# A gMLP and linear-attention block on one NeuronCore: the spatial matmul u = w_sp z2 by Strassen's seven products over half of the source tiles

## The chip, the cores and the metric

The kernel runs on one core of a Trainium2 chip. The metric is the device time in microseconds (us), here that of the one core, as the median of several runs. The core has five engines that matter here, each with its own queue of instructions worked off in order: PE (TensorE, matmuls; its weight loads are shown apart as PEld), DVE (VectorE), ACT (ScalarE), POOL (GpSimd) and SP (SyncE), which in this kernel issues the DMA transfers. An instruction starts when those ahead of it on its engine are through and the semaphores it waits for have arrived.

## The reference

The block has two halves: linear attention over 2048 tokens with 512 features, then a gated MLP that mixes tokens. Both add to the token stream x, with shifts, scales and gates from a condition. The change lies in the second half:

```python
S, D, F = 2048, 512, 1376; Fh = F // 2          # 688
z  = gelu(einsum("bsd,df->bsf", x, w_in))
z1 = z[..., :Fh]
z2 = layernorm(z[..., Fh:], axis=-1)
g  = einsum("ts,bsf->btf", w_sp, z2) + b_sp[None, :, None]
y  = einsum("bsf,fd->bsd", z1 * g, w_out)
...
x = x + gb * y
```

`w_sp` is 2048 x 2048 in tokens, so g is a 2048 x 2048 by 2048 x 688 product, the largest of the block.

## The kernel before

Tokens are cut into 16 tiles of 128 (NT), the 688 features of z2 into two halves of 344 (HB). The kernel computes in fp32 by splitting each operand into a high part of the type fp32r and a low part, the remainder, and by adding three matmuls: high x high, high x low, low x high. The helper `hi_lo` makes them: ACT copies into the high part (L83), and DVE or POOL subtracts it from the source for the low part (L84). `mm3` issues the three output matmuls (L66 to L68).

The first 349 us compute the attention half and z. Their instructions stand in an order of some hundreds of named steps (the string ORDER) that `run_all` works off; it ends with the z2 tiles and the first splits of w_sp. z1 goes to a DRAM buffer (z1d) and the token stream to another (x1d); z2 stays in SBUF, one tile of [128, 2, 688] (high, low) for each token tile (`Z2`).

Then comes the w_sp stage, a loop over the 16 target tiles. For target tile i, `sp_mm` (L769) multiplies, for all 16 source tiles s, the 128 x 128 block w_sp[i, s] (transposed in the input, split in groups of four blocks by `split_wsp`) with z2 of tile s: three matmuls for each half of the features, 96 of 344 columns in all, into one PSUM tile of two banks that stays open for the whole sum. `u_out` (L780) adds the bias and multiplies with z1 on DVE. `u_x` (L809) cuts the result into two uint16 planes on ACT (L194) and sends them through a transposing DMA; `u_e` (L814) puts the planes together on DVE (L204) and splits high (ACT, L818) and low parts (DVE, L819, L820). `wout_mm` (L842) multiplies with w_out in 17 matmuls of 512 columns, and `out_store` (L837) adds the token stream on DVE and stores. In the loop the output product of tile i-1 stands behind the w_sp matmuls of tile i, and `load3(i + 1)`, `u_e(i - 1)` and the splits of w_sp's tile i+1 in the middle of them (L847 to L888). The last tile is transposed on PE (`u_t`, L789) in place of the DMA, between two pieces of the output product of tile 14.

w_out itself is prepared in iteration 0: `load_wout` fetches six pieces, `split_wout` (L755) multiplies each with the gate on DVE (L757) and splits it on ACT and POOL.

SBUF comes from fixed pools, each a ring of equal buffers: `ws` 2 of 5504 fp32, `zs` 16 of 1376 (the z2 tiles), `s4` 8 of 1024 (split w_sp), `md` 4, `ta` 6, `tb` 7 of 768. PSUM has three pools of two tiles: `b` (two banks each), `t` and `o`. All stay open for the whole kernel. A pool's next tile waits until the readers of the one it replaces are through.

## Time and profile before

Times are device microseconds; the profiled execution is one run of its own beside the timed ones.

| | us |
|---|---|
| median of 3 runs | 663.76 (661.69 to 666.0) |
| profiled execution, its own time | 662.32 |
| its span, first to last instruction | 660.5 |
| DVE busy | 360.2 (55%) |
| ACT busy | 288.9 (44%) |
| POOL busy | 264.1 (40%) |

The profile page gives the busy time of each engine with its share of the span and the count of instructions; the chain that ended last by engine and by line; and groups of instructions, each with its line, engine and operation, what is written and read (`out<-in`, buffer numbers left out), shape and count, then the busy time and the mean duration of one in ns, and behind the second bar the engine's idle time just ahead of them with what ended most of it. Matmuls overlap: a group's mean can be longer than the distance from one to the next, and for rates the distance counts. A timeline gives a row for each stretch of equal instructions on an engine: start, length, engine, line, operation, shape, count, and in brackets the wait ahead of it and its releaser. A row of the windows view gives a stretch of time, its length and for PE, weight loads, DVE, ACT and POOL the busy time with the count, then the granted clock of PE, the share of the DMA engines and GB/s. The names `z`, `u`, `us`, `uc`, `uth`, `utl`, `pout` in the rows are the tiles of the lines above.

### The profile page before, as it was taken

The page shows a single profiled execution, that of the slowest core. Times are in us where ns is not written, and L with a number is a line of the kernel's source. Part 1 is how long each engine was busy: PE and PEld are TensorE (multiplying, and loading weights), DVE is VectorE, ACT ScalarE, POOL GpSimd, SP SyncE. Part 2 cuts the span into 40 slices and gives each one's busy share as a digit, 9 for nine tenths or more (in the row PEclk, how much of TensorE's full clock was granted, in tenths as well). Part 3 has the DMA queues.
Part 4 walks back from the last instruction along what each step waited for, and adds up shares of the span by engine and source line. Part 5 has one row for each costly group of instructions (what it writes and reads, how often), then busy time and mean ns, then how long its engine had stood idle before and what let it go on. Part 6 is the DMA issues. An engine that isn't in the chain of part 4 may idle for free.

```text
span 660.5 us, 9681 instructions
## 1 busy us (share of the span) xinstructions
PE 648.7 (98%) x3697; PEld 599.9 (91%) x3697; DVE 360.2 (55%) x628; ACT 288.9 (44%) x477; POOL 264.1 (40%) x237
## 2 busy tenths in 40 slices
PE   8999999999998999999999989999999999999998
PEld 8988888888787999999999989999999999999997
DVE  6879888777888977966761543122323322222222
ACT  4877655655646456664646233122122221221210
POOL 1444125165973546614467834233333022333300
PEclk9999999999999999999999999999999999999999
...
GB/s 308 158 81 17 80 110 56 69 105 88 22 101 112 171 133 150 166 191 156 107 75 203 119 140 175 90 105 112 141 140 142 141 97 96 105 128 141 78 40 33
DMA packets 77358, 77.32 MB, mean 117 GB/s; under 512 B 54176, under 2 KB 54688, under 8 KB 77312
## 3 DMA queue, kind: packets, MB, share of 16 engines
...
## 4 chain that ended last, share of the span: by engine, by line
PE 84%; DVE 6%; POOL 3%; ACT 3%; DMA 2%; issue 2%; SPq 0%; POOLq 0%; DVEq 0%; ACTq 0%
PE u L777 32%; PE z L568 16%; PE pout L68 3%; PE pout L67 3%; PE pout L66 3%; PE g L66 2%; PE g L68 2%; PE g L67 2%; PE kp L68 2%; PE kp L66 2%; PE kp L67 2%; PE warm L113 2%; PE qp L68 2%; PE qp L67 2%; PE qp L66 2%
## 5 line engine op out<-in xcount | busy, mean ns | idle before, releaser
L777 PE MATMUL u<-z,wsp 128*128 128x344 f32 x1536 | 244.7, 320 | 0.0
L777 PEld LDWEIGHTS u<-z,wsp 128*128 128x128 f32 x1536 | 243.1, 188 | 1.3
L84 POOL TENSOR_TENSOR wsp<-raw_wsp,wsp 128x512 fp32r<-128x512 f32 x64 | 82.8, 1321 | 173.1 <-ACT wsp L83 171.2
L568 PE MATMUL z<-win,ht 128*128 128x344 f32 x768 | 123.4, 320 | 2.0 <-ACT ht L83 1.9
L568 PEld LDWEIGHTS z<-win,ht 128*128 128x128 f32 x768 | 121.5, 188 | 3.7 <-ACT ht L83 2.2
L194 ACT COPY upl<-us 128x768 uint16<-128x768 uint16 x30 | 23.5, 830 | 128.8 <-DVE us L786 117.3
L180 POOL TENSOR_TENSOR mv<-ve,mhalf 128x1 f32<-128x1 f32 x48 | 33.8, 715 | 110.8 <-DVE ve L179 103.9
L784 DVE SCALAR_TENSOR_TENSOR us<-u,bsp,z1r 128x688 f32<-128x688 f32 x16 | 15.0, 934 | 112.5 <-PE u L777 112.5
L818 ACT ACTIVATE uth<-uc 128x768 fp32r<-128x768 f32 x15 | 12.7, 846 | 77.0 <-DVE uc L204 77.0
L204 DVE COPY uc<-uplt 128x768 uint16<-128x768 uint16 x30 | 17.7, 647 | 39.0 <-DMA uplt<-upl 39.0
L83 ACT ACTIVATE wsp<-raw_wsp 128x512 fp32r<-128x512 f32 x64 | 35.2, 616 | 0.0
L66 PE MATMUL pout<-wout,uth 128*128 128x512 f32 (+1 forms) x85 | 32.2, 379 | 1.9 <-ACT uth L818 1.9
L839 DVE TENSOR_TENSOR o<-x,pout 128x512 f32<-128x512 f32 (+1 forms) x17 | 11.2, 657 | 40.4 <-PE pout L832 40.4
L68 PE MATMUL pout<-wout,utl 128*128 128x512 f32 (+1 forms) x85 | 32.2, 379 | 0.2 <-DVE utl L819 0.2
L67 PE MATMUL pout<-wout,uth 128*128 128x512 f32 (+1 forms) x85 | 32.1, 378 | 0.0
L598 POOL TENSOR_TENSOR z<-zz,z 128x688 fp32r<-128x688 f32 x16 | 27.7, 1740 | 7.3 <-ACT z L595 7.3
L390 POOL TENSOR_TENSOR pksum<-pksum,tk 128x512 f32<-128x512 f32 x15 | 22.5, 1499 | 16.6 <-DVE tk L362 15.2
L497 POOL TENSOR_TENSOR prod<-pq,zrep 128x512 f32<-128x512 f32 x16 | 22.3, 1404 | 11.6 <-ACT zrep L617 4.8
L66 PE MATMUL po<-m,pt 128*128 128x512 f32 x64 | 25.3, 396 | 1.1 <-DVE xr L544 1.1
L66 PE MATMUL qp<-wq,ht 128*128 128x512 f32 x64 | 25.6, 401 | 0.0
L68 PE MATMUL po<-m,pt 128*128 128x512 f32 x64 | 25.4, 396 | 0.2 <-POOL pt L224 0.2
L66 PE MATMUL g<-pkhl,hhl 128*128 128x512 f32 x64 | 25.5, 399 | 0.0
...
## 6 DMA issues: line engine op xcount, KB each, us to landing
raw_wsp<-in_w_sp SPq DMA_DIRECT2D x32, 512.0 KB, 6.0
raw_mod<-in_w_mod SPq DMA_DIRECT2D x12, 512.0 KB, 5.3
...
```

The lines of the kernel that those rows point to most:

```text
L66: mm(o, a_hi, b_hi, start=first, stop=False, **kw)
L67: mm(o, a_hi, b_lo, start=False, stop=False, **kw)
L68: mm(o, a_lo, b_hi, start=False, stop=last, **kw)
L83: nc.scalar.activation(hi, src, AF.Copy)
L84: (lo_eng or nc.vector).tensor_sub(lo, src, f(hi))
L180: nc.gpsimd.tensor_tensor(mv[:, 1:2], ve, mhalf, op=OP.pow)
L194: nc.scalar.copy(pl[:, h], v[:, :, h])
L390: nc.gpsimd.tensor_add(pksum, pksum, PK[t])
L497: nc.gpsimd.tensor_mul(pr, PQ[t], KV["z"])
L568: mm(p[:, b, :HB], a[:, i, kc], win[h][:, j, kc, b * HB:(b + 1) * HB], start=kc == 0 and k == 0, stop=kc == KC - 1 and k == 2)
L598: nc.gpsimd.tensor_sub(Z2[t][:, 1], ZZ.pop(t), f(Z2[t][:, 0]))
L777: mm(p[:, n, :HB], a[:, i, s % 4], b[:, j, n * HB:(n + 1) * HB], start=s == 0 and k == 0, stop=s == NT - 1 and k == 2)
```

## The change

Target tiles are taken in pairs (t0, t1), and the feature halves as two columns, so that a pair is a 2 x 2 block product for each pair of source blocks. For pairs 1 to 7 the sources 0 to 7 and 8 to 15 are treated apart: source tiles 0 to 7, as four pairs (2j, 2j+1), go by Strassen's scheme in Winograd's form, seven products P1 to P7 in place of eight, and source tiles 8 to 15 stay plain. Pair 0 is plain throughout.

The right sides of the seven products (the forms) are made once, by `t_forms(j)` for j = 0 to 3: POOL adds the high and low parts of z2's tiles 2j and 2j+1 back together (`te`, `to`), DVE makes three differences, and a fourth in place, each is split again (ACT high, DVE low) into new tiles or, for P7, over the second half of z2's tile 2j. The left sides are made for each pair by `s_sums` (four sums of w_sp blocks on DVE) and `s_split` (ACT high, POOL low). `prod` is one product: 4 blocks x 3 = 12 matmuls of 344 columns into one bank; `plain` adds the sources 8 to 15 to a bank, 24 matmuls of 344 columns, or 15 and 9. `c_early` and `c_late` combine the banks on ACT and DVE; the product with z1 (`u_mul`) and the fill of the last columns (`u_fill`) become instructions of their own. A pair's splits of plain w_sp blocks fall from eight to four.

The pools `ws`, `ta`, `tb` and the PSUM pools are closed behind the ORDER part. Five new pools and a PSUM pool of eight single banks with fixed roles are opened in their place, with waits kept for each tile (`reuse_waits="tile"`). In the ORDER string the splits sw0,2 and sw0,3 are replaced by sw1,0 and sw1,1, and ls1 (the load of w_sp's tile 1) stands later; the splits of the second halves of tiles 0 and 1 come behind the last z2 tile. The output sum is written over the tile of the token stream. The last pair's two tiles are both transposed on PE, tile 15 in two parts.

```diff
-        "ws": ([P, 5504], 2), "zs": ([P, 1376], 16), "s4": ([P, 1024], 8), "st": ([P, 1024], 4),
-        "md": ([P, 512], 4), "ta": ([P, 512], 6), "tb": ([P, 768], 7),
+    sizes = {"zs": ([P, 1376], 16), "s4": ([P, 1024], 8), "st": ([P, 1024], 4), "md": ([P, 512], 4)}
+    sizes2 = {"ws": ([P, 5504], 2), "ta": ([P, 512], 6), "tb": ([P, 768], 7)}
+    sizes3 = {"tq": ([P, 688], 12), "wo": ([P, 3072], 2), "u": ([P, 768], 4), "c": ([P, 344], 3), "xo": ([P, 512], 2)}
...
+    early.close()
+    pools.update({k: late.enter_context(tc.tile_pool(name=k, bufs=n, reuse_waits="tile")) for k, (_, n) in sizes3.items()})
+    psp = late.enter_context(tc.tile_pool(name="psp", bufs=1, space=PSUM, reuse_waits="tile"))
+    def bank(k, name, shape=(P, 512)):
+        return psp.tile(list(shape), F32, tag=f"bank{k}", name=name)
...
     def load_wout(k):
-        r = sb("ta", [P, D], F32, f"raw_wout{k}")
+        r = sb("xo", [P, D], F32, f"raw_wout{k}")
...
+    def t_forms(j):
+        a, b = Z2[2 * j], Z2[2 * j + 1]
+        e = sb("u", [P, FH], F32, f"te{j}")
+        o = sb("u", [P, FH], F32, f"to{j}")
+        nc.gpsimd.tensor_add(e, f(a[:, 0]), f(a[:, 1]))
+        nc.gpsimd.tensor_add(o, f(b[:, 0]), f(b[:, 1]))
+        t2 = sb("c", [P, HB], F32, f"t2_{j}")
+        lo_, hi_ = slice(0, HB), slice(HB, FH)
+        def parts(dst, src):
+            nc.scalar.activation(dst[:, 0], src, AF.Copy)
+            nc.vector.tensor_sub(dst[:, 1], src, f(dst[:, 0]))
+        t1, t2r, t4 = (sb("tq", [P, 2, HB], F32R, f"t{k}_{j}r") for k in (1, 2, 4))
+        nc.vector.tensor_sub(e[:, lo_], e[:, hi_], e[:, lo_])
+        parts(t1, e[:, lo_])
+        nc.vector.tensor_sub(t2, o[:, hi_], e[:, lo_])
+        parts(t2r, t2)
+        nc.vector.tensor_sub(o[:, lo_], o[:, lo_], t2)
+        parts(t4, o[:, lo_])
+        nc.vector.tensor_sub(e[:, hi_], o[:, hi_], e[:, hi_])
+        parts(a[:, :, hi_], e[:, hi_])
+        TB[j] = {"P5": t1, "P6": t2r, "P4": t4, "P7": a[:, :, hi_], "P1": a[:, :, lo_], "P2": b[:, :, lo_],
+                 "P3": b[:, :, hi_]}
+    def s_sums(p, part):
+        q = [RAW["wsp", 2 * p + i, 0].rearrange("p (a b) c -> p a b c", b=2) for i in range(2)]
+        a11, a12, a21, a22 = q[0][:, :, 0], q[0][:, :, 1], q[1][:, :, 0], q[1][:, :, 1]
+        if part == 0:
...
+            nc.vector.tensor_sub(s3, a11, a21)
+            nc.vector.tensor_add(a21, a21, a22)
+            nc.vector.tensor_sub(s2, a21, a11)
+            SA[p] = {"P1": a11, "P2": a12, "P4": a22, "P5": a21, "P6": s2, "P7": s3, "S2": s2}
+        else:
+            s4 = sb("md", [P, 4, P], F32, f"s4_{p}")
+            nc.vector.tensor_sub(s4, a12, SA[p].pop("S2"))
+            SA[p]["P3"] = s4
+    def s_split(p, k):
+        SF[p, k] = sb("s4", [P, 2, 4, P], F32R, f"f{k}_{p}")
+        s = SA[p].pop(k)
+        nc.scalar.activation(SF[p, k][:, 0], s, AF.Copy)
+        nc.gpsimd.tensor_sub(SF[p, k][:, 1], s, f(SF[p, k][:, 0]))
+    BANK = {"P1": 0, "P5": 1, "P6": 2, "P7": 3, "P2": 4, "P3": 5, "P4": 6, "R": 7}
+    def prod(p, k, last=True):
+        B[p, k] = bank(BANK[k], f"{k}_{p}")
+        a = SF.pop((p, k))
+        for j in range(4):
+            b = TB[j][k]
+            for n, (x_, y_) in enumerate(((0, 0), (0, 1), (1, 0))):
+                mm(B[p, k][:, :HB], a[:, x_, j], b[:, y_], start=j == 0 and n == 0,
+                   stop=last and j == 3 and n == 2)
...
+    def c_early(p, k):
...
+            nc.scalar.activation(C[p, 1], B.pop((p, "P1"))[:, :HB], AF.Copy)
...
+            nc.vector.tensor_add(C[p, 2], B.pop((p, "P6"))[:, :HB], C[p, 1])
...
+            nc.vector.tensor_add(C[p, 3], B.pop((p, "P7"))[:, :HB], C[p, 2])
...
+    def u_mul(t, c0=0, c1=FH):
+        nc.vector.tensor_mul(U[t][:, c0:c1], U[t][:, c0:c1], Z1[t][:, c0:c1])
...
-        o = sb("ta", [P, c1 - c0], F32, f"o{t}_{c0}")
-        nc.vector.tensor_add(o, X3[t][:, c0:c1], PO[t][:, c0:c1])
+        o = X3[t][:, c0:c1]
+        nc.vector.tensor_add(o, o, PO[t][:, c0:c1])
         dma(out[t * P:(t + 1) * P, c0:c1], o)
...
+    load_wout(0)
+    load_wout(1)
+    for i in range(2):
+        for h in range(2):
+            plain(0, ("P2", "P3", "P4", "R")[2 * i + h], i, h, 0, 8, True, False)
+    for i in range(2):
+        for k in (2, 3):
+            split_wsp(i, k)
+    for t in (2, 3):
+        load_wsp(t)
+    for j in range(4):
+        t_forms(j)
+        if j < 3:
+            split_wout(2 * j)
+            split_wout(2 * j + 1)
+            if j < 2:
+                load_wout(2 * j + 2)
+                load_wout(2 * j + 3)
+    for i in range(2):
+        load_z1(i)
+        for h in range(2):
+            plain(0, ("P2", "P3", "P4", "R")[2 * i + h], i, h, 8, NT, False, True)
+    s_sums(1, 0)
+    for k in ("P1", "P6", "P7"):
+        s_split(1, k)
+    for i in range(2):
...
+        u_fill(i)
+        u_x(i)
+    for p in range(1, NT // 2):
+        t0, t1 = 2 * p, 2 * p + 1
+        prod(p, "P1")
+        c_early(p, "P1")
+        s_split(p, "P5")
+        prod(p, "P6")
+        c_early(p, "P6")
+        s_split(p, "P2")
+        u_e(t0 - 2)
+        load_x3(t0 - 2)
+        prod(p, "P7")
+        c_early(p, "P7")
+        s_sums(p, 1)
+        prod(p, "P5")
+        c_early(p, "P5")
+        s_split(p, "P3")
+        wout_mm(t0 - 2)
+        u_e(t1 - 2)
+        load_x3(t1 - 2)
+        s_split(p, "P4")
+        prod(p, "P2", False)
+        split_wsp(t0, 2)
+        prod(p, "P3", False)
+        split_wsp(t0, 3)
+        prod(p, "P4", False)
+        split_wsp(t1, 2)
+        wout_mm(t1 - 2)
+        load_z1(t0)
+        load_z1(t1)
...
+            load_wsp(t0 + 2)
+            load_wsp(t1 + 2)
+        plain(p, "P2", 0, 0, 8, NT, False, True)
+        split_wsp(t1, 3)
+        c_late(p, 0, 0)
+        plain(p, "P3", 0, 1, 8, NT, False, True)
+        c_late(p, 0, 1)
+        u_mul(t0)
+        u_fill(t0)
...
+            u_x(t0)
+            s_sums(p + 1, 0)
+            s_split(p + 1, "P1")
+        plain(p, "P4", 1, 0, 8, NT, False, True)
+        c_late(p, 1, 0)
...
+            s_split(p + 1, "P6")
...
+        plain(p, "R", 1, 1, 8, 13, True, False)
...
+        plain(p, "R", 1, 1, 13, NT, False, True)
+        c_late(p, 1, 1)
...
+            u_mul(t1)
+            u_fill(t1)
+            u_x(t1)
+            s_split(p + 1, "P7")
```

Three places show how the instructions now stand. In the rows a name carries its tile's number behind the last underscore; `wout1` is the low part of w_out, `raw_wout` the fetched piece, `fP1_1` the split left form of P1 for pair 1.

POOL at the start of the w_sp stage, before: the splits of w_sp's tile 1, the splits of w_out, and then the splits of tile 2.

```order
L598 TENSOR_TENSOR z2_15_3781<-zz_15_3712,z2_15_3781 128x688
L84 TENSOR_TENSOR wsp1_0_3784<-raw_wsp_1_0_3257,wsp1_0_3784 128x512
L84 TENSOR_TENSOR wsp1_1_3787<-raw_wsp_1_0_3257,wsp1_1_3787 128x512
L84 TENSOR_TENSOR wsp1_2_3790<-raw_wsp_1_1_3259,wsp1_2_3790 128x512
L84 TENSOR_TENSOR wsp1_3_3793<-raw_wsp_1_1_3259,wsp1_3_3793 128x512
L84 TENSOR_TENSOR wout1_3720<-raw_wout0_3725,wout0_3719 128x512
L84 TENSOR_TENSOR wout1_3720<-raw_wout1_3727,wout0_3719 128x512
L751 MEMSET raw_wout5_3808 128x512
```

The same place now, from the last split of w_sp ahead of the forms on:

```order
L86 TENSOR_TENSOR wsp1_3_3872<-raw_wsp_1_1_3558,wsp1_3_3872 128x512
L790 TENSOR_TENSOR te0_3883<-z2_0_3212 128x688
L791 TENSOR_TENSOR to0_3884<-z2_1_3078 128x688
L86 TENSOR_TENSOR wout1_3744<-raw_wout0_3759,wout0_3743 128x512
L86 TENSOR_TENSOR wout1_3744<-raw_wout1_3761,wout0_3743 128x512
L790 TENSOR_TENSOR te1_3913<-z2_2_2804 128x688
L791 TENSOR_TENSOR to1_3914<-z2_3_2761 128x688
L86 TENSOR_TENSOR wout1_3744<-raw_wout2_3909,wout0_3743 128x512
L86 TENSOR_TENSOR wout1_3744<-raw_wout3_3911,wout0_3743 128x512
L764 MEMSET raw_wout5_3941 128x512
L790 TENSOR_TENSOR te2_3945<-z2_4_3262 128x688
L791 TENSOR_TENSOR to2_3946<-z2_5_3014 128x688
```

Between every two sets of te and to now stand two splits of w_out; form 3 and the splits `fP1_1`, `fP6_1`, `fP7_1` follow behind them.

DVE at the same place, before: the statistics of the last z tile, then w_out's products with the gate and the outcome of target tile 0.

```order
L590 SCALAR_TENSOR_TENSOR zb_3778<-mv2_3773 128x1
L757 TENSOR_TENSOR raw_wout0_3725<-raw_wout0_3725,mod5_3709 128x512
L757 TENSOR_TENSOR raw_wout1_3727<-raw_wout1_3727,mod5_3709 128x512
L784 SCALAR_TENSOR_TENSOR us0_3876<-u0_3733,bsp_98,z1r0_3721 128x688
L786 COPY us0_3876<-us0_3876 128x64
L757 TENSOR_TENSOR raw_wout2_3729<-raw_wout2_3729,mod5_3709 128x512
```

And DVE there now, form 0 and the start of form 1:

```order
L592 SCALAR_TENSOR_TENSOR zb_3753<-mv2_3748 128x1
L800 TENSOR_TENSOR te0_3883<-te0_3883 128x344
L797 TENSOR_TENSOR t1_0r_3888<-te0_3883,t1_0r_3888 128x344
L802 TENSOR_TENSOR t2_0_3887<-to0_3884,te0_3883 128x344
L797 TENSOR_TENSOR t2_0r_3889<-t2_0_3887,t2_0r_3889 128x344
L804 TENSOR_TENSOR to0_3884<-to0_3884,t2_0_3887 128x344
L797 TENSOR_TENSOR t4_0r_3890<-to0_3884,t4_0r_3890 128x344
L806 TENSOR_TENSOR te0_3883<-to0_3884,te0_3883 128x344
L797 TENSOR_TENSOR z2_0_3212<-te0_3883,z2_0_3212 128x344
L770 TENSOR_TENSOR raw_wout0_3759<-raw_wout0_3759,mod5_3709 128x512
L770 TENSOR_TENSOR raw_wout1_3761<-raw_wout1_3761,mod5_3709 128x512
L800 TENSOR_TENSOR te1_3913<-te1_3913 128x344
```

Eight subtractions of a form now stand ahead of the two products with the gate, and these ahead of the next form.

ACT from one target tile to the next late in the stage, before: the splits of a w_sp tile, the planes of the tile just done, then the high part of the one before.

```order
L83 ACTIVATE wsp14_3_5816<-raw_wsp_14_1_5666 128x512
L194 COPY upl13_5887<-us13_5883 128x768 x2
L818 ACTIVATE uth13_5957<-uc13_5954 128x768
L83 ACTIVATE wsp15_0_5962<-raw_wsp_15_0_5819 128x512
L83 ACTIVATE wsp15_1_5965<-raw_wsp_15_0_5819 128x512
```

ACT at the border of pairs 6 and 7 now (`p1s` is the copy of P1's bank, `fP7_7` the left form of P7 for pair 7):

```order
L832 ACTIVATE fP6_7_6067<-s2_7_6035 128x512
L196 COPY upl13_6098<-us13_5855 128x768 x2
L832 ACTIVATE fP7_7_6103<-s3_7_6034 128x512
L875 ACTIVATE p1s_7_6119<-P1_7_6106 128x344
L832 ACTIVATE fP5_7_6121<-raw_wsp_15_0_5970 128x512
L832 ACTIVATE fP2_7_6139<-raw_wsp_14_0_5966 128x512
L946 ACTIVATE uth12_6145<-uc12_6142 128x768
L832 ACTIVATE fP3_7_6188<-s4_7_6167 128x512
L946 ACTIVATE uth13_6214<-uc13_6211 128x768
L832 ACTIVATE fP4_7_6221<-raw_wsp_15_0_5970 128x512
```

The high part of P7's left form now stands behind the planes of the pair's second tile, and that of P4 behind the high part of tile 13.

227 lines of the change are left out of this document (126 added, 101 removed).

## The prediction

> **What bounds the kernel now.** First the page's busy times and its chain of work, then PE's timeline where the w_sp stage begins, then the other engines there.
>
> ```profile
> PE 648.7 (98%) x3697; PEld 599.9 (91%) x3697; DVE 360.2 (55%) x628; ACT 288.9 (44%) x477; POOL 264.1 (40%) x237
> PE 84%; DVE 6%; POOL 3%; ACT 3%; DMA 2%; issue 2%; SPq 0%; POOLq 0%; DVEq 0%; ACTq 0%
> L777 PE MATMUL u<-z,wsp 128*128 128x344 f32 x1536 | 244.7, 320 | 0.0
> 349.38 30.43 PE L777 MATMUL u<-z,wsp 128*128 128x344 f32 x192
> 381.74 0.50 PE L66 MATMUL pout<-wout,uth 128*128 128x512 f32 x1 [1.92 <-ACT uth L818]
> 386.22 15.30 PE L777 MATMUL u<-z,wsp 128*128 128x344 f32 x96
> 401.36 0.39 PE L66 MATMUL pout<-wout,uth 128*128 128x512 f32 x1
> 405.24 15.30 PE L777 MATMUL u<-z,wsp 128*128 128x344 f32 x96
> 421.00:459.00 38.00, 38.00 (x228) 36.63 (x227) 10.00 (x15) 8.99 (x14) 10.41 (x10) 1.00 0.42 123
> ```
>
> PE is busy 98% of the span and carries 84% of the chain. In the w_sp stage the 1536 matmuls of L777 never wait (idle 0.0). A token tile is 96 of them in 401.36 - 386.22 = 15.14 us, 157.7 ns each, and then 17 output matmuls in 405.24 - 401.36 = 3.88 us: 19.02 us a tile, 38.04 a pair. The last row is one such pair (PE, weight loads, DVE, ACT, POOL, granted clock, DMA share, GB/s): PE is full, the three helpers are busy 10.0, 9.0 and 10.4 us of 38. So the helpers have room on average. What decides is whether they deliver in time, in their own orders.
>
> **The change, part by part.** *Matmuls.* A pair had 192 matmuls of 344 columns; now 84 in the seven products and 96 plain, 180. At 157.7 ns that is 28.39 us, with two output products of 3.88 a pair of 36.15 instead of 38.04: 1.89 less, 13.2 us over seven pairs. The output matmuls already accumulate one after the other in one bank and take 228 ns for 512 columns, so that all matmuls of a product go to one bank costs nothing that these rows show.
>
> *The start of pair 0.*
>
> ```profile
> 352.22 0.73 ACT L579 ACTIVATE zz<-z 128x688 f32<-128x688 f32 x1
> 361.11 1.69 POOL L598 TENSOR_TENSOR z<-zz,z 128x688 fp32r<-128x688 f32 x1 [2.14 <-ACT z L595]
> 362.76 5.05 POOL L84 TENSOR_TENSOR wsp<-raw_wsp,wsp 128x512 fp32r<-128x512 f32 x4
> 371.16 0.52 POOL L751 MEMSET raw_wout<- 128x512 f32 x1
> 379.49 0.86 POOL L760 MEMSET wout<- 64x512 f32 x1
> ```
>
> The first bank of P2 lies where the last z tile was, so PE, free at 349.38, waits for ACT's read of it (the order of waits says so), which ended at 352.95. Pair 0 is still 192 matmuls, 30.28 us: PE is through at 383.3.
>
> *The forms.* In the same time POOL, DVE and ACT make the four sets of forms. POOL's row: after the four splits (362.76 to 367.81, 1.26 each) come te0 and to0, then two splits of w_out, then te1, to1 and so on, and only behind to3 the split of pair 1's first left form. DVE's row: the eight subtractions of form j stand ahead of the two products w_out x gate, and POOL's w_out splits need those through ACT. So POOL stands at its w_out split until DVE and ACT are through with form j, and te of form j+1 stands behind that split. The loop is serial. The durations:
>
> ```profile
> L407 DVE TENSOR_TENSOR raw_wo<-raw_wo,mod 128x512 f32<-128x512 f32 x4 | 2.7, 685 | 0.0
> L175 DVE BATCH_NORM_STATS2 bst<-zz 128x6 f32<-128x344 f32 x2 | 0.9, 510 | 7.4 <-ACT zz L579 7.4
> L839 DVE TENSOR_TENSOR o<-x,pout 128x256 f32<-128x256 f32 x2 | 0.8, 422 | 3.0 <-PE pout L832 3.0
> L801 ACT ACTIVATE uth<-ut 128x128 fp32r<-128x128 f32 x1 | 0.3, 270 | 0.0
> L83 ACT ACTIVATE wout<-raw_wout 128x512 fp32r<-128x512 f32 x6 | 3.4, 620 | 0.9 <-DVE raw_wout L757 0.9
> 378.44 2.37 DVE L204 COPY uc<-uplt 128x768 uint16<-128x768 uint16 x2 [2.66 <-DMA uplt<-upl]
> 380.84 0.84 ACT L818 ACTIVATE uth<-uc 128x768 fp32r<-128x768 f32 x1 [4.40 <-DVE uc L204]
> 381.79 0.83 DVE L819 TENSOR_TENSOR utl<-uc,uth 128x640 fp32r<-128x640 f32 x1 [0.98 <-ACT uth L818]
> L390 POOL TENSOR_TENSOR pksum<-pksum,tk 128x512 f32<-128x512 f32 x15 | 22.5, 1499 | 16.6 <-DVE tk L362 15.2
> ```
>
> No row is a DVE subtraction of 344 columns: bounds 0.42 (256) and 0.69 (512); I take 0.50, by the 344-column statistics (0.51). ACT's 344-column copy lies between 0.27 (128) and 0.62 (512): 0.47. A hand-over is 0.03 from DVE to ACT and 0.11 back (the 378.44, 380.84 and 381.79 rows). A form has four triples of subtraction, ACT's high part and DVE's low part: 0.50 + 0.03 + 0.47 + 0.11 + 0.50 + 0.03 = 1.64, four 6.56. Then product 0.69, hand-over 0.03, ACT 0.62, hand-over 0.1: 1.44. Then POOL: two splits 2.52, te and to 2 x 1.69 = 3.38 (by L598; at the rate of L390 it would be 2.0 each, the upper end). One round is 13.9 us. te0 starts at 367.81, to0 ends at 371.2, three rounds and both memsets (0.52, 0.86) give to3's end at 414.3. Form 3 needs three triples, a subtraction, a hand-over and ACT's last high part, 5.92, and behind it ACT's first left form 0.62: P1 of pair 1 starts at 420.8. PE stands from 383.3 to 420.8, 37.5 us; the 1.9 us wait at 381.74 and the one at 352.95 lie inside that. With all bounds the one way P1 starts near 409, the other way near 431.
>
> One term in it is the first subtraction of a form while POOL still adds o.
>
> ```profile
> 364.72 0.94 DVE L784 SCALAR_TENSOR_TENSOR us<-u,bsp,z1r 128x688 f32<-128x688 f32 x1 [4.35 <-PE u L777]
> 365.69 0.93 DVE L786 COPY us<-us 128x64 f32<-128x64 f32 x1
> 402.53 0.20 DVE L786 COPY us<-us 128x64 f32<-128x64 f32 x1
> L820 DVE TENSOR_TENSOR uth<-uc,uth 48x128 fp32r<-48x128 f32 x15 | 18.1, 1209 | 0.5
> ```
>
> The same 64-column copy takes 0.20 alone and 0.93 under POOL's split, ending with it; L820, 48x128, takes 1.2 beside POOL's splits. So I let that subtraction end with to, and the whole form count behind it. Were there no such block, the first triple (1.64) would lie beside to: four times less, P1 at 414.2, and 6.6 us off the sum. The Trainium skill, SBUF - State Buffer, Who interferes with whom, says that a DVE instruction with two SBUF inputs contends with GpSimd's reads and that the loser blocks for the whole instruction; by that rule the sum stands as worked out.
>
> *Pair 1.* Its helpers start late too.
>
> ```profile
> 401.56 0.93 DVE L784 SCALAR_TENSOR_TENSOR us<-u,bsp,z1r 128x688 f32<-128x688 f32 x1 [4.00 <-PE u L777]
> 387.65 1.57 ACT L194 COPY upl<-us 128x768 uint16<-128x768 uint16 x2 [3.88 <-POOL us L782]
> 393.34 1.09 DVE L204 COPY uc<-uplt 128x768 uint16<-128x768 uint16 x2 [6.23 <-DMA uplt<-upl]
> L818 ACT ACTIVATE uth<-uc 128x768 fp32r<-128x768 f32 x15 | 12.7, 846 | 77.0 <-DVE uc L204 77.0
> uplt<-upl SPq DMA_TRANSPOSE x15, 3.7
> ```
>
> From P1's start: three 512-column sums on DVE 2.1, ACT 0.7, POOL's two low parts of P6 and P7 to 5.4; ACT's plane copies of tiles 0 and 1 wait for POOL's memsets behind those and end at 8.7; P1's copy 0.47 and P5's high part 0.62 behind them, POOL's low part 1.3: P5's third matmul at 11.2. SP can send tile 0's transpose at 7.1; it lands 3.7 to 4.9 later, then 1.1 + 0.9 + 0.9 to the low part that the third output matmul needs: 14.9. The output product ends at 18.3 instead of 11.45, 6.8 late. With the P4 wait below pair 1 lasts 43.7.
>
> *Pairs 2 to 7.* Two places. At the border DVE's add for the last tile starts 0.2 after R ends (as 401.56 does after 401.36), then 0.5, the 688-column product 0.88 (the 640-column row and a little), the fill 0.2, ACT's two plane copies 1.57, P7's high part 0.62 and POOL's low part 1.3 behind them: 5.5, where PE's third P7 matmul is due at 2 x 1.89 + 0.32 = 4.1. 1.4 us. After the first output product DVE adds (0.2 + 0.69), copies tile t1's transpose (1.09), ACT makes its high part (0.9) and then P4's (0.6), POOL the low part (1.4): 4.9 against 3.78 + 0.32. 0.8 us. So a pair takes 36.15 + 2.2 = 38.35: no gain is left. Ends: 36.15 if both hide, some 40 if the POOL block adds one DVE step at each place.
>
> *The end.*
>
> ```profile
> 648.62 0.39 PE L66 MATMUL pout<-wout,uth 128*128 128x512 f32 x1
> 649.99 0.60 PE L793 MATMUL ut<-ident,us 128*128 128x128 f32 x4
> 650.43 0.27 PE L795 MATMUL ut<-ident,us 128*128 128x128 f32 x1
> ```
>
> From the first output matmul behind the last w_sp matmul to the end of the span (660.5) it is 11.9 us, and it stays so. Eight transposes of 0.11 (four from 649.99 to 650.43) move in front of it: 0.9.
>
> *Covered.* The left forms' high parts replace w_sp splits one for one. The form tiles, P2's and P3's left forms and the split of w_sp's other half lie beside matmuls. The moved loads of w_sp come behind the last z products' needs by the order; their cover is PE's 15 us on sources 0 to 7. If it fails, PE waits there, inside the wait before 420.8, at no cost.
>
> *Sum.* 420.8 + 43.7 + 6 x 38.35 + 0.9 + 11.9 = 707.4 us of span. The profiled execution took 662.3, 1.8 more than its span: 709.2. That is 46.9 more than before: 39.1 at the transition (420.8 against 381.74) and 7.8 behind it (274.7 us up to the end part, against 648.62 - 381.74 = 266.9). The median of the runs shown, 663.8, lies 0.2% above the profiled execution.
>
> **The rivals.**
>
> ```profile
> GB/s 308 158 81 17 80 110 56 69 105 88 22 101 112 171 133 150 166 191 156 107 75 203 119 140 175 90 105 112 141 140 142 141 97 96 105 128 141 78 40 33
> 7.00:14.00 7.00, 5.88 (x51) 5.72 (x52) 5.30 (x10) 3.07 (x7) 0.55 (x1) 1.00 1.01 401
> raw_wsp<-in_w_sp SPq DMA_DIRECT2D x32, 512.0 KB, 6.0
> ```
>
> A. *The helpers keep ahead of PE, and the saved matmuls show.* For it: some 10 us of work on each helper in 38. If PE never waited, pair 1 would start at 383.3 and each pair take 36.15: 383.3 + 253.1 + 0.9 + 11.9 + 1.8 = 651.0, faster by 1.7%. It breaks even when pair 1 starts at 394.6. Against it: that leaves 11.3 us after PE's pair 0 for what three rounds of 13.9 must do, so a round would have to take 5.2, less than POOL's own 5.9 in it.
>
> B. *POOL alone sets the pace.* Its 5.9 a round, with DVE and ACT hidden, would bring P1 to 397.0 and the end to 685.4 (664.6 if the pairs do not wait either). Against it: the products by the gate stand behind the form in DVE's row, so POOL cannot run ahead. Only much shorter DVE and ACT steps than any row shows would do it.
>
> C. *The loads for the next pair come late.* SP sends tile t1's output, both z1 tiles and the four w_sp loads only when the second output product is done, some 24 us into the pair; the sums for the next P6 need 2.5 MB of that. At 401 GB/s it takes 6 us, at the 6.0 us shown for a load some 10: both in time for 36. If the queue ran at 141 GB/s (the highest of the last slices in the first row, the w_sp stage, which is demand and not a limit) it would take 17.6, P6 would be 5 us late in each pair, and the end at 741.
>
> **How the numbers follow.** The worked-out case, a serial loop of forms and small waits in each pair, 0.74; A 0.05, B 0.08 (half of what is left of it near 665, half near 685), C 0.10, others 0.03. The time is that of the first: 709. Its own ends: P1 at 409 with clean pairs gives 409 + 41 + 6 x 36.15 + 14.6 = 681; P1 at 431 with pairs of 39.5 gives 726. 684 to 728 leaves out A, C and most of B, and a little of the first case: 2 in 10. The runs before spread from 661.7 to 666.0, so about 1% is what can be told from no change. Faster by over 1% is A, 0.05; within 1% the lower half of B, 0.04; slower all the rest, 0.91.
>
> **What would show it.** In the changed profile PE stands idle from about 383 to about 420, with POOL's first P1 split, or ACT's part of it, as what ends the wait; te0 to te3 start some 14 us apart on POOL, with POOL idle between to and the w_out split, waiting for ACT. Pair 1 takes 44 us, later pairs 38 to 39, with PE waiting before P7 for POOL and before P4. The matmul groups of the stage sum to 1452 instead of 1536 instructions. Wrong it would be if te's follow at 6 us, if PE's idle time at the transition is under 10 us, or if a pair takes 36.2.

## The result, and the profile after

The changed kernel takes 717.5 us (median of four runs, 715.9 to 720.0), the kernel before 664.6 beside it: a ratio of 1.081, 95% interval 1.075 to 1.086. It is slower by some 53 us; 709 were predicted, 684 to 728 as the range.

The page of the changed kernel first: busy times, the chain that ended last, PE's granted clock in 40 slices, and the largest groups of the new w_sp stage.

```profile
PE 651.4 (91%) x3619; PEld 592.9 (83%) x3619; DVE 434.1 (61%) x746; ACT 311.4 (44%) x521; POOL 307.7 (43%) x266
PE 63%; DVE 14%; issue 8%; POOL 7%; ACT 7%; DMA 2%; SPq 0%; ACTq 0%; POOLq 0%; DVEq 0%
PEclk9999999999999999999999559999999999999999
L854 PE MATMUL P<-z,wsp 128*128 128x344 f32 x648 | 104.9, 323 | 3.4 <-ACT zz L581 3.4
L844 PE MATMUL P<-z,fP 128*128 128x344 f32 x336 | 60.8, 331 | 41.7 <-ACT fP L832 36.3
```

PE's share fell from 98% to 91% of a longer span, its part of the chain from 84% to 63%, and DVE's rose to 14%. The matmul groups of z tiles with the left forms (L844) carry 41.7 us of idle time, and two slices of the clock row stand at half. Where it is, PE's timeline shows:

```profile
352.48 0.40 PE L165 MATMUL pmod<-yh,ones 128*128 128x512 f32 x1
356.54 13.12 PE L854 MATMUL P<-z,wsp 128*128 128x344 f32 x72 [3.44 <-ACT zz L581]
373.29 11.47 PE L854 MATMUL P<-z,wsp 128*128 128x344 f32 x72
...
421.18 0.94 PE L844 MATMUL P<-z,fP 128*128 128x344 f32 x2 [32.63 <-ACT fP L832]
422.94 3.23 PE L844 MATMUL P<-z,fP 128*128 128x344 f32 x10 [0.82 <-POOL fP L833]
...
466.11 2.05 PE L844 MATMUL P<-z,fP 128*128 128x344 f32 x12
...
471.00 0.58 PE L844 MATMUL P<-z,fP 128*128 128x344 f32 x2 [0.95 <-ACT fP L832]
472.35 1.85 PE L844 MATMUL P<-z,fP 128*128 128x344 f32 x10 [0.78 <-POOL fP L833]
...
484.85 0.42 PE L844 MATMUL P<-t_0r,fP 128*128 128x344 f32 x1 [0.69 <-POOL fP L833]
```

Behind pair 0 PE stands 32.6 us until the first left form of pair 1 is there. That form is late because ACT and DVE still make the four sets of right forms. The first round of them on POOL, DVE and ACT:

```profile
371.16 1.67 POOL L790 TENSOR_TENSOR te<-z 128x688 f32<-128x688 f32 x1
372.79 1.67 POOL L791 TENSOR_TENSOR to<-z 128x688 f32<-128x688 f32 x1
372.86 1.97 DVE L800 TENSOR_TENSOR te<-te 128x344 f32<-128x344 f32 x1 [10.31 <-POOL te L790]
...
380.45 1.28 DVE L770 TENSOR_TENSOR raw_wout<-raw_wout,mod 128x512 f32<-128x512 f32 x2
381.88 2.55 POOL L86 TENSOR_TENSOR wout<-raw_wout,wout 128x512 fp32r<-128x512 f32 x2 [7.42 <-ACT wout L85]
384.38 1.66 POOL L790 TENSOR_TENSOR te<-z 128x688 f32<-128x688 f32 x1
```

That is the loop of the prediction: te and to, the form on DVE and ACT (372.86 to 380.45), the product by the gate, ACT's high part, POOL's two splits after waiting 7.42 us for it, and only then the next te, 13.2 us after the first. The other rounds take 13.7 and 13.8.

Set against the prediction, in us:

| step | predicted | measured |
|---|---|---|
| P1 of pair 1 | 420.8 | 421.18 (417.6 without the 3.56 by which z ends later) |
| one round of the forms | 13.9; with a memset in it 14.4 and 14.8 | 13.2; with a memset in it 13.7 and 13.8 |
| pair 1 | 43.7 | 466.11 - 421.18 = 44.93 |
| pairs 2 to 6, mean (starts 466.11 to 661.77) | 38.35 | 39.13 |
| pair 7 with the transposes | 39.25 | 40.20 |
| from the first matmul of the last two output products | 11.9 | 12.2 |
| span | 707.4 | 714.2 |

Of the 53.7 us of span, 35.9 are the transition (417.6 against 381.74), 13.9 pairs 1 to 7 (280.8 up to the end part, against 266.9), 0.3 the end, and 3.56 lie ahead of the w_sp stage: z's end (the 352.48 row) stands at 348.92 before, and between 350.1 and 352.5 in the profiles of all variants below, whose matmuls up to there are the same. How much of the 3.56 the change itself brings is not shown.

### The profile page after: what moved, and what is told of

Its sections match the earlier page's. It is cut to its first block, busy times and chain, and to the rows that moved or that the text cites. A ratio compares the mean times of both kernels' runs of the same rounds, so it can differ in the third digit from the quotient of the medians.

```text
span 714.2 us, 9688 instructions
## 1 busy us (share of the span) xinstructions
PE 651.4 (91%) x3619; PEld 592.9 (83%) x3619; DVE 434.1 (61%) x746; ACT 311.4 (44%) x521; POOL 307.7 (43%) x266
## 4 chain that ended last, share of the span: by engine, by line
PE 63%; DVE 14%; issue 8%; POOL 7%; ACT 7%; DMA 2%; SPq 0%; ACTq 0%; POOLq 0%; DVEq 0%
PE z L570 15%; PE P L854 11%; PE R L854 4%; DVE uc L206 3%; POOL fP L833 3%; PE warm L115 2%; PE kp L69 2%; PE kp L68 2%; PE kp L70 2%; PE g L68 2%; PE P L844 2%; PE g L70 2%; PE g L69 2%; PE qp L70 2%; PE qp L68 2%
## 5 line engine op out<-in xcount | busy, mean ns | idle before, releaser
L854 PE MATMUL P<-z,wsp 128*128 128x344 f32 x648 | 104.9, 323 | 3.4 <-ACT zz L581 3.4
L854 PEld LDWEIGHTS P<-z,wsp 128*128 128x128 f32 x648 | 103.8, 191 | 4.5 <-ACT zz L581 3.9
L844 PE MATMUL P<-z,fP 128*128 128x344 f32 x336 | 60.8, 331 | 41.7 <-ACT fP L832 36.3
L844 PEld LDWEIGHTS P<-z,fP 128*128 128x128 f32 x336 | 54.8, 193 | 46.6 <-ACT fP L832 38.3
L833 POOL TENSOR_TENSOR fP<-raw_wsp,fP 128x512 fp32r<-128x512 f32 x28 | 42.8, 1538 | 109.6 <-ACT fP L832 109.6
L833 POOL TENSOR_TENSOR fP<-s,fP 128x512 fp32r<-128x512 f32 x21 | 27.0, 1285 | 54.9 <-ACT fP L832 54.9
L86 POOL TENSOR_TENSOR wsp<-raw_wsp,wsp 128x512 fp32r<-128x512 f32 x36 | 46.0, 1305 | 1.1 <-ACT wsp L85 1.1
L854 PE MATMUL R<-z,wsp 128*128 128x344 f32 x216 | 35.8, 321 | 0.0
L854 PEld LDWEIGHTS R<-z,wsp 128*128 128x128 f32 x216 | 34.2, 188 | 0.0
L70 PE MATMUL pout<-wout,utl 128*128 128x512 f32 (+1 forms) x85 | 32.6, 384 | 0.3 <-DVE utl L932 0.3
L832 ACT ACTIVATE fP<-s 128x512 fp32r<-128x512 f32 x21 | 13.1, 629 | 36.5 <-DVE s L822 19.5
```

The lines of the kernel that those rows point to most:

```text
L70: mm(o, a_lo, b_hi, start=False, stop=last, **kw)
L86: (lo_eng or nc.vector).tensor_sub(lo, src, f(hi))
L833: nc.gpsimd.tensor_sub(SF[p, k][:, 1], s, f(SF[p, k][:, 0]))
L844: mm(B[p, k][:, :HB], a[:, x_, j], b[:, y_], start=j == 0 and n == 0, stop=last and j == 3 and n == 2)
L854: mm(B[p, k][:, :HB], a[:, x_, s % 4], b[:, y_], start=first and s == s0 and n == 0, stop=last and s == s1_ - 1 and n == 2)
```

## The experiments

Each kernel starts from the changed one unless said otherwise; the ratio is to the kernel before, run beside it. They stand as 1 to 4, 6 to 8, then 5 and 9 to 11, which build on each other. 1, 4, 6 and 7 are on the start of the stage, 2, 5 and 9 on the border between pairs, 3 on PE's clock, 8 and 10 join several, and 11 starts the seven products later.

**1. The products by the gate out of the loop.** All six pieces of w_out are loaded at once into the form tiles, multiplied ahead of the last z2 tile's normalisation, and split by ACT and DVE ahead of the forms.

```diff
-        r = sb("xo", [P, D], F32, f"raw_wout{k}")
+        r = sb("tq", [P, D], F32, f"raw_wout{k}")
...
-        hi_lo(wo2[0][:, k], wo2[1][:, k], r, lo_eng=nc.gpsimd)
+        hi_lo(wo2[0][:, k], wo2[1][:, k], r)
...
+    for k in range(6):
+        gate_wout(k)
     z2_norm(NT - 1)
...
+    for k in range(6):
+        split_wout(k)
     for j in range(4):
         t_forms(j)
-        if j < 3:
-            split_wout(2 * j)
-            split_wout(2 * j + 1)
```

> The six splits of w_out are taken out of the loop of forms: all six pieces are fetched at once, the products with the gate, the high parts and (now on DVE) the low parts stand ahead of form 0. Serial-loop theory: in the changed kernel a round takes 13.2 to 13.8 us because te of form j+1 stands on POOL behind w_out splits that need DVE and ACT to be through with form j. Without them a round is what DVE takes for a form, 7.6 us (380.45 - 372.86), so P1 of pair 1 starts near 403 to 409 instead of 421.2 (409 if POOL's te and to, now made during the form before, block some DVE steps longer) and the time is 699.5 to 705.5. Rival (the forms' own work, the w_sp loads or ACT set P1's start and w_out only fills gaps): P1 stays at 418 to 421 and the time within 3 us of 717.5.

711.3 us (1.073, 1.069 to 1.077): 6 us faster, not the 12 or more of the theory. DVE's rows of this kernel:

```profile
355.50 6.70 DVE L770 TENSOR_TENSOR raw_wout<-raw_wout,mod 128x512 f32<-128x512 f32 x5
368.91 7.24 DVE L86 TENSOR_TENSOR wout<-raw_wout,wout 128x512 fp32r<-128x512 f32 x6 [4.51 <-ACT wout L85]
378.54 1.96 DVE L803 TENSOR_TENSOR te<-te 128x344 f32<-128x344 f32 x1 [2.40 <-POOL te L793]
...
410.08 0.52 DVE L800 TENSOR_TENSOR z<-te,z 128x344 fp32r<-128x344 f32 x1 [0.61 <-ACT z L799]
```

The loop is broken: four forms run from 378.54 to 410.6, 8 us each, where a round was 13.2 to 13.8. But they start 8 us later as counted from z's end (378.54 against 372.86, z ending 2.3 earlier here): a product and a low part now take 1.2 to 1.3 us each beside POOL's splits (6.70 for five, 7.24 for six), where two products took 1.28. What was moved still had to be done ahead of the first product. P1 of pair 1 starts at 410.62 all the same, 10.6 earlier than in the change and close to the 403 to 409 that were expected. The rest is lost behind it. In the profiled run, which took 714.7 us, pair 1 takes 46.7, and of the next five pairs two take 39.0 and 39.1 and three 41.0 to 41.3. In these three PE's clock fell to half behind the waits ahead of P7:

```profile
462.09 0.58 PE L847 MATMUL P<-z,fP 128*128 128x344 f32 x2 [0.84 <-ACT fP L835]
463.44 2.52 PE L847 MATMUL P<-z,fP 128*128 128x344 f32 x10 [0.77 <-POOL fP L836]
```

**2. P7's left form ahead of the planes, P4's ahead of uth.**

```diff
             s_split(p + 1, "P6")
+            s_split(p + 1, "P7")
...
-            s_split(p + 1, "P7")
...
+        s_split(p, "P4")
         u_e(t1 - 2)
         load_x3(t1 - 2)
-        s_split(p, "P4")
```

> Only the order of two left forms is changed: P7's split of the next pair stands ahead of the plane copies of the pair's second tile, and P4's ahead of the high part of the tile's transpose. Theory: the waits ahead of P7 and P4 are queueing behind those copies; a pair falls from 39.1 us (mean of pairs 2 to 6) to 36.2 to 36.6, 6 pairs give 15 to 18 us and pair 1 loses its P4 wait of 0.9: the time is 698 to 703. Rival (the helpers' work is what is late, and the wait moves: planes later by 0.6 us, then the output product or P5 waits): a pair stays above 38 and the time above 709.

709.6 us (1.070, 1.068 to 1.072). The waits ahead of P7 and P4 are gone, as the theory said, but a pair takes 37.8 to 38.4 and not 36.3: P5's third matmul now waits some 1.0 us for POOL in every pair from 2 on. That the waits go is the theory's part; the time and the pairs are the rival's.

**3. PE kept busy through the wait.** 130 extra matmuls of 512 columns into an unused bank, between pair 0 and pair 1.

```diff
+    wt = bank(3, "wt")
+    for k in range(130):
+        mm(wt, ones, Z2[NT - 1][:, 0, :512], start=True, stop=True)
     s_sums(1, 0)
```

> 130 matmuls of 512 columns into a bank that is free are added where PE stands still, behind pair 0's last matmul; their result is not used. Clock theory: the matmuls behind the 32.6 us of idle time run at half rate (10 of them in 3.23 us, granted clock 0.50 from 421.2 to 426.0) because the clock was lowered while PE stood; with PE busy until about 418 the clock there is 1.0, the ten take 1.9 us or less, and the time falls by 1.4 us, or by up to 2.9 if P5's half rate goes too. Rival (first use of new operands or of the first bank is slow whatever the clock): the ten still take over 3 us at a clock of 1.0. If the 130 matmuls take longer than 32 us P1 starts later by the difference.

718.4 us, one run. The stretches of PE's wait, with the busy times of PE, weight loads, DVE, ACT and POOL, and the granted clock behind them:

```profile
418.70:421.30 2.60, 0.07 (x1) 0.00 (x0) 1.47 (x4) 1.50 (x3) 0.00 (x0) 1.00 0.00 0
421.30:426.00 4.70, 3.57 (x12) 3.23 (x13) 4.60 (x6) 1.15 (x2) 2.64 (x2) 0.54 0.00 0
```

The clock stood at 1.00 up to 421.3, and still the ten matmuls of P1 take 3.23 us, at 0.54: the 2.6 us without matmuls at the end of the dummy work (and 1.1 more behind P1's first two) were enough. So neither the theory nor the rival: the clock does explain the slow matmuls, but work that ends early does not keep it. The 1.4 us on P1 do not reach the time, since PE waits 2.34 us in this kernel ahead of the first output product; the 32 us themselves are the wait for the form.

**4. All four subtractions of a form ahead of its four low parts.** DVE then doesn't wait for ACT after each of them.

```diff
         nc.vector.tensor_sub(e[:, lo_], e[:, hi_], e[:, lo_])
-        parts(t1, e[:, lo_])
         nc.vector.tensor_sub(t2, o[:, hi_], e[:, lo_])
-        parts(t2r, t2)
         nc.vector.tensor_sub(o[:, lo_], o[:, lo_], t2)
-        parts(t4, o[:, lo_])
         nc.vector.tensor_sub(e[:, hi_], o[:, hi_], e[:, hi_])
+        parts(t1, e[:, lo_])
+        parts(t2r, t2)
+        parts(t4, o[:, lo_])
         parts(a[:, :, hi_], e[:, hi_])
```

> Inside a form the four subtractions that make the differences now stand ahead of the four low parts on DVE, so that ACT's high parts lie beside them; w_out stays in the loop. Theory (DVE and ACT work one after the other in a triple, and the round is serial): a form falls from 7.6 us to about 5.6 (four subtractions 3.5 with the long first one, four low parts 2.1), a round from 13.7 to 11.6, P1 starts near 413 and the time is 709 to 710. Rival (POOL alone sets the pace of the loop): a round stays above 13 and the time above 715.

705.3 us (1.066, 1.060 to 1.072). A form falls from 7.6 us to 5.24, as DVE's rows show:

```profile
370.55 1.97 DVE L800 TENSOR_TENSOR te<-te 128x344 f32<-128x344 f32 x1 [10.25 <-POOL te L790]
...
375.37 0.51 DVE L797 TENSOR_TENSOR z<-te,z 128x344 fp32r<-128x344 f32 x1
375.79 1.28 DVE L770 TENSOR_TENSOR raw_wout<-raw_wout,mod 128x512 f32<-128x512 f32 x2
```

The time is some 4 us below the 709 to 710 of the theory, which took 5.6 for a form. te now starts every 10.9 to 11.4 us and P1 at 408.80, 12.4 earlier; 2.3 of it is z's end in this profile, 7.1 are the three rounds, 3.0 what stands behind the last te. Shortening one step of the loop pays once for each turn, with nothing given back: that is what a serial loop does, and the rivals of the prediction (POOL alone sets the pace, or the helpers run ahead) would not.

**6. Pair 1's plain part ahead of its seven products**, so that PE has work during the forms; pair 1's w_sp splits go between the forms.

```diff
+        t_adds(j)
+        split_wsp(2 + j // 2, 2 + j % 2)
         t_forms(j)
...
+    for i in range(2):
+        for h in range(2):
+            plain(1, ("P2", "P3", "P4", "R")[2 * i + h], i, h, 8, NT, True, (i, h) == (1, 1))
     s_sums(1, 0)
```

> Forms, w_out and left forms stay as in the changed kernel; pair 1's 96 plain matmuls (15.1 us) are put ahead of its products, into the time in which PE waits for the forms, with their four splits of w_sp in POOL's waiting time, and pair 2's w_sp and z1 loads are sent earlier since pair 1's plain part no longer covers them. Theory (what costs is that PE has no other work while the forms are made): PE's wait falls from 32.6 to 16 to 19 us, P1 of pair 1 stays at 421 to 424, and the time is 702 to 705. Rival (pair 1 needed its plain part as cover for pair 2's loads and left forms): PE waits 4 to 10 us at pair 2's P1 and the time is 706 to 713.

723.1 us (1.091, 1.088 to 1.094), slower than the change itself: neither theory. PE's row says why.

```profile
424.08 6.14 PE L863 MATMUL P<-z,wsp 128*128 128x344 f32 x22 [37.87 <-DVE us L877]
```

The plain sums of pair 1 go to the four PSUM banks that still hold pair 0, and these are read by `c_plain`, which stands behind all the forms in DVE's row. The work was there for PE, the banks were not: a flaw of this kernel's design, and a wait that neither side of the expectation had listed.

**7. `to` ahead of `te` on POOL**, so that the first subtraction can't run beside POOL's second sum.

```diff
-        nc.gpsimd.tensor_add(e, f(a[:, 0]), f(a[:, 1]))
         nc.gpsimd.tensor_add(o, f(b[:, 0]), f(b[:, 1]))
+        nc.gpsimd.tensor_add(e, f(a[:, 0]), f(a[:, 1]))
```

> Only the order of POOL's two adds in a form is turned round: to ahead of te. DVE's first subtraction needs te alone, so nothing runs on POOL beside it any more. Contention theory (the first subtraction takes 1.95 us instead of 0.51 because POOL's second add holds it off): it starts 1.65 us later and takes 0.5, ends at about the same time (within 0.4 us), rounds stay at 13.2 to 14.2 and the time within 3 us of 717.5. Rival (the first subtraction costs 1.95 us by itself, as first use of te or by its operands): it still takes 1.9, each round is 1.6 longer, and P1 starts 6 to 7 us later: 723 to 725.

716.0 us, one run, within 2 us of the change. The first subtraction on DVE:

```profile
372.41 0.52 DVE L800 TENSOR_TENSOR te<-te 128x344 f32<-128x344 f32 x1 [11.92 <-POOL te L791]
```

It now starts behind both sums and takes 0.52; in the change it starts beside the second sum, takes 1.97, and ends 0.4 us behind it. Rounds stay at 13.3 to 13.9. So the 1.45 us are waiting, as the prediction had assumed when it let the subtraction end with to. The Trainium skill, SBUF - State Buffer, Who interferes with whom, says that a DVE instruction with two SBUF inputs contends with a GpSimd instruction that reads SBUF, for a port pair that one of them locks; these two rows agree.

**8. Experiments 1, 4 and 6 together, the border's moves of 2 and 5, and pair 0 in banks that z has left**, so that PE need not wait 3.4 us for ACT.

```diff
+    for k in (2, 3, 4, 5, 0, 1, 6, 7):
+        bank(k, f"first{k}")
...
+    for k in (0, 1, 2, 3, 4, 5):
+        gate_wout(k)
...
+        if j > 0:
+            t_adds(j)
+        if j > 1:
+            split_wsp(j, 2)
+            split_wsp(j, 3)
         t_forms(j)
```

> All cures together: subtractions of a form ahead of its low parts; gate products of w_out ahead of the forms and its splits behind form 0 with the low part on DVE; te0 and to0 ahead of the last z2 low part; pair 1's plain part first; left forms of P7, P5 and P4 ahead of the copies; and the banks of pair 0 laid where PE need not wait for the last z tile. If PE never waits, it starts u at about 349 to 353, pair 0 takes 30.3, seven pairs 36.33 each, the transposes 0.9, the end 12.2 and 1.8 around the span: 649 to 653, 1.6 to 2.2% faster than before. Theory with its known losses (DVE and POOL hold each other off while forms are made, some 1 to 5 us at P1 or P6 of pair 1, up to 0.4 a pair): 652 to 659. Rival (DVE and POOL work strictly one at a time, so that the forms end 8 us or more behind pair 1's plain part, or the saving is given back in pair 2): 662 or more, no faster than before.

700.0 us (1.056, 1.053 to 1.058). The wait of 3.44 is gone (PE starts w_sp at 352.12), but the time is far above the 652 to 659 of the theory: the cures get in each other's way. Its two longest waits of PE, as total, times and longest:

```profile
PE P L866 <- DVE us L880: 19.8, 1, 19.8
PE pout L68 <- ACT uth L958: 8.5, 5, 2.0
```

The gate products ahead of everything take 10.37 us for six beside POOL, w_sp's splits come late and PE waits for them inside pair 0, the banks of pair 0 hold pair 1 up again, and a new wait stands ahead of the output products. Many cures at once told little.

**5. Experiment 2, and P5's left form ahead of the planes too.**

```diff
             s_split(p + 1, "P7")
+            s_split(p + 1, "P5")
...
-        s_split(p, "P5")
+        if p == 1:
+            s_split(p, "P5")
```

> As e2_left_ahead, and P5's left form of the next pair is also split ahead of the plane copies of the pair's second tile. In e2 the wait moved to P5: its third matmul is 1.2 us late in each pair (PE's row at 509.67), and a pair takes 38.0 instead of 36.3 (28.4 for 180 matmuls and 2 x 3.97 for the output products, as the rows there have it). Theory (queueing behind the copies, now for P5): the wait goes, a pair takes 36.3 to 36.7, six pairs give 8 to 10 us against e2: 699 to 702. Rival (there is always a next one: P2's split or the second tile's transpose becomes late): a pair stays above 37.3 and the time above 705.

710.8 us (1.070, 1.066 to 1.074), no better than experiment 2. The wait moved on once more (the row counts pair 1 too):

```profile
PE pout L68 <- ACT uth L946: 10.9, 7, 2.0
```

No product from pair 2 on waits any more, but the first output product of each pair does, for the high part of the token tile it multiplies. That part hangs on DVE's merge of the transposed planes, which stands in DVE's row behind P6's addition, and so behind P1's copy on ACT, and so behind the planes. Pairs 2 and 5 take 37.8 and 38.3 us; pairs 3, 4 and 6, where the granted clock fell behind this wait (last section), 40.2 to 40.6. The rival is right up to here.

**9. Experiment 5, and that merge moved ahead of R's addition at the pair's end.**

```diff
+        if p == 1:
+            u_e(t0 - 2)
-        u_e(t0 - 2)
...
         plain(p, "R", 1, 1, 13, NT, False, True)
+        if p + 1 < NT // 2:
+            u_e(t0)
         c_late(p, 1, 1)
```

> All of the last experiment's moves (P7's and P5's left forms ahead of the planes, P4's ahead of uth), and DVE's merge of tile t0's transpose (with ACT's high part and the low part) moved from behind P6's addition of the next pair to ahead of R's addition at the end of this pair. Theory (what is left at the border is a queue of finite length, and its last piece is that merge): the waits ahead of P7, P5, P4 and of the first output product are all under 0.5 us, pairs 2 to 7 take 36.3 to 36.8 us instead of 39.1, pair 1 and the start stay: 717.5 - 6 x 2.6 = 702 us, 700 to 704. Rival (removing a wait only shows a next one): R's addition and the planes of tile t1 are now later by the merge, some product of the next pair waits for them, pairs stay at 37.8 or more, 708 to 712 us.

697.3 us (1.050, 1.047 to 1.053). All of PE's waits from 465 to 690 us, which is pairs 2 to 7, and then one pair from output product to output product, with the busy times in it:

```profile
PE P L844 <- POOL fP L833: 0.3, 1, 0.3
PE pout L70 <- DVE utl L932: 0.3, 1, 0.3
```

```profile
481.05:517.65 36.60, 36.56 (x216) 34.59 (x215) 19.87 (x27) 11.27 (x20) 15.86 (x13) 1.00 0.45 128
```

From pair 2 on PE has nothing to wait for, and a pair takes 36.6 where it took 39.13. So the chain of waits at the border was finite, and its pieces were all late work of one kind, queued behind the planes. Only now the 12 saved matmuls of a pair show: 38.04 before, 36.6 here. It is a little faster than the theory's 700 to 704; 1.9 us of the difference in span is z, which ended earlier in this profile.

**10. Experiments 4 and 9 together.**

> The four subtractions of a form ahead of its low parts, and all moves at the pair border of the kernel above together. Theory (the two losses are independent: one at the transition, one at each border): the gain of the subtractions (717.5 - 705.3 = 12.2 us) and that of the border add up: 690 us, 687 to 693. Rival (a border's waits come from the late start of pair 1, so that they shrink with it, and gains overlap): 694 to 700 us. Neither makes it as fast as the kernel before: P1 of pair 1 would have to start some 26 us earlier still.

688.6 us (1.037, 1.034 to 1.039), inside the theory's range: the two losses add. Pairs 2 to 6 take 36.2 to 36.3 here. What is left is the start, PE's wait ahead of pair 1:

```profile
411.17 0.94 PE L844 MATMUL P<-z,fP 128*128 128x344 f32 x2 [22.57 <-ACT fP L832]
```

**11. The seven products from pair 2 on.** Experiment 9's border, with pairs 0 and 1 both made the plain way, in banks of their own. The sums of the forms move from POOL to DVE (experiment 4's order within a form), and P7's form goes to a tile `t7` until pair 1 has read z2. The w_sp loads go by halves, w_out's preparation is spread over both plain pairs, and pair 0 takes banks that z has left, as in experiment 8.

```diff
-        nc.gpsimd.tensor_add(e, f(a[:, 0]), f(a[:, 1]))
-        nc.gpsimd.tensor_add(o, f(b[:, 0]), f(b[:, 1]))
+        t7 = sb("md", [P, HB], F32, f"t7_{j}")
+        nc.vector.tensor_add(e, f(a[:, 0]), f(a[:, 1]))
+        nc.vector.tensor_add(o, f(b[:, 0]), f(b[:, 1]))
...
-            B[p, k] = bank(BANK[k], f"{k}_{p}")
+            B[p, k] = bank(BANK[k] - 4 * (p == 1), f"{k}_{p}")
...
+    pair(0, 0, 8)
...
+    t_sums(0)
+    t_parts(0)
+    pair(0, 8, NT)
...
+    t_sums(1)
+    t_parts(1)
+    pair(1, 0, 8)
...
+    pair(1, 8, NT)
...
+    wout_mm(0)
+    wout_mm(1)
-    for p in range(1, NT // 2):
+    for p in range(2, NT // 2):
```

> The border moves of the last experiment, and the seven products begin one pair later: token pairs 0 and 1 are both made the plain way (192 matmuls each, in banks 4 to 7 and 0 to 3), pairs 2 to 7 by the seven products. The forms are made wholly on DVE and ACT (sums of the halves on DVE instead of POOL) between 353 us and the start of pair 2, P7's form in a tile of its own until pair 1's matmuls on sources 0 to 7 have read z2. Theory (the loss was the start of the product alone: no PE work stood beside the forms; and the saved matmuls show once the border is clear): the time before, 663.8, less 6 pairs x (38.04 - 36.6), and 0.9 for the transposes at the end: 656 us, 654 to 660, the first of the kernels here that is faster than before. Rival (the helpers cannot do the forms, pair 0's and pair 1's merges, w_out's and w_sp's splits in some 65 us, since DVE and POOL hold each other off): PE waits 5 to 10 us ahead of the first output product or of P1 of pair 2, at half the clock for 5 us more: 664 to 672 us.

655.7 us (655.0 to 656.5; the kernel before 663.6 beside it): a ratio of 0.988, 0.986 to 0.990. It is the only kernel of the study that is faster than the one before, by 1.2%, and it lies where the theory put it (654 to 660). Its PE rows (with "..." for the rows between) and its waits:

```profile
414.14 0.50 PE L68 MATMUL pout<-wout,uth 128*128 128x512 f32 x1 [0.96 <-ACT uth L949]
...
422.47 2.06 PE L847 MATMUL P<-z,fP 128*128 128x344 f32 x12
...
517.57 11.48 PE L857 MATMUL P<-z,wsp 128*128 128x344 f32 x72
553.69 11.48 PE L857 MATMUL P<-z,wsp 128*128 128x344 f32 x72
```

```profile
PE pout L68 <- ACT uth L949: 1.0, 1, 1.0
PE P L847 <- POOL fP L836: 0.8, 1, 0.8
PE pout L70 <- DVE utl L935: 0.3, 1, 0.3
PE pout L70 <- DVE utl L950: 0.2, 1, 0.2
```

PE waits 2.3 us in all behind z. From 517.57 to 553.69 a pair takes 36.12, the prediction's floor of 36.15. The helpers do what held up pair 1 before, beside the 192 plain matmuls of pair 0 and the 192 of pair 1, 352.6 to 413 us: P1 of the first pair with seven products starts at 422.47, about where it does in the change (421.18), but with pair 1 already done. The loss at the start of the stage was not the scheme and not its work on the helpers, which is all still there, now on DVE and ACT; it was that no matmuls stood beside that work. This kernel changes several things at once, and what the sums on DVE, the banks and the spread loads each add is not shown.

## Why the prediction was right

**The serial loop at the start** carried most of it and was right in mechanism and in size. The waits are in the profile as described (POOL 7.42 us for ACT's high part of w_out), and a round was 0.7 to 1.0 us shorter than worked out: from the end of to0 to the product by the gate the form took 5.99 us instead of 6.56. Experiment 4 shows the loop: 2.4 us off each form moved P1 by 10 us. Experiment 1 shows that the preparation of w_out was what tied POOL to the form: without it four forms run at 8 us each. That the first subtraction takes until to is over was one assumption in it; experiment 7 shows it.

**Pairs 2 to 7** were right in that no gain is left, and too short by 0.8 us each. The prediction named the waits ahead of P7 and P4, 2.2 us together. In pair 2 P7's third matmul was due at 470.20, five matmuls behind the 469.41 where P6's last three start, and starts at 472.35: 2.15 late instead of 1.4; P4's third is 0.85 late: 3.0. An output product takes 3.97 where 3.88 was taken: 36.33 + 3.0 = 39.3. In pair 3 P7's third matmul is 1.39 late, as forecast, and that pair takes 38.74. What differs is the 688-column product on DVE in front of the planes, here in pairs 3 and 4:

```profile
506.32 0.88 DVE L910 TENSOR_TENSOR us<-us,z1r 128x688 f32<-128x688 f32 x1
540.79 0.69 DVE L820 TENSOR_TENSOR s<-raw_wsp,raw_wsp 128x512 f32<-128x512 f32 x1 [2.11 <-DMA raw_wsp<-in_w_sp]
545.06 1.68 DVE L910 TENSOR_TENSOR us<-us,z1r 128x688 f32<-128x688 f32 x1
```

In pair 4 it stands beside POOL's low part of P6 (544.72 to 546.01) and takes 1.68 instead of 0.88; P7's third matmul is 2.2 late, and the pair takes 39.51. POOL is later there because DVE's first sum for P6 waits 2.11 us for a load of w_sp; in pair 3 it waits 1.25. The prediction gave the block by POOL as its upper end for these places, and took the loads to be in time. That the load decides is read from these rows; no run moves the load alone.

What the prediction did not say is that these two waits stood for a whole queue: removing them (2) gave 1.0 us a pair and the next (5) nothing more, until the last piece (9) let the pair fall to 36.6. A cure priced by the two waits alone would have been mis-sized.

**Pair 1** was 1.2 us too short, **the end** 0.3. In pair 1 the three sums on DVE were taken as 2.1 us and took 3.1, since the second stood beside POOL's low part of P1 and took 1.64 where the others took 0.7:

```profile
421.79 1.64 DVE L821 TENSOR_TENSOR raw_wsp<-raw_wsp 128x512 f32<-128x512 f32 x1
```

What hangs on them, down to the output product, came later by nearly as much: its third matmul starts 15.7 us behind P1 instead of 14.9. The clock, which the prediction left out, is not the reason: P1's ten matmuls do take 3.23 us behind the long wait, where the same count in pair 2 takes 1.85 (the 422.94 and 472.35 rows), but in experiment 9, where the clock is back at full speed before P5, PE waits 1.4 us ahead of the first output matmul, and that starts 14.9 us behind P1 in both.

**The rivals.** That the helpers keep ahead (651 us) and that POOL alone sets the pace (685) are out by the rounds. Late loads as rival C had them, with P6 some 5 us late in each pair, are out: no wait of PE in the stage names a DMA. But DVE's first sum waits 1.3 to 2.1 us for w_sp's load in each pair from 2 on, and this reaches PE through the 688-column product, as above. The price of the helpers that keep ahead was right for a kernel whose helpers do keep ahead from pair 2 on: experiment 11 took 655.7, with six of the seven pairs.

**Sum.** The span came out at 714.2 against 707.4. Of the 6.8, pair 1 to the end give 6.4 (1.2, five times 0.8, 0.95 and 0.3) and P1's start the rest: 0.4, from a z that ended 3.56 later in this profile and a transition 3.2 shorter than predicted. That these two nearly cancel is luck; the transition by itself was 35.9 us where 39.1 were forecast.
